# One PSUM tile with named banks, k projected by 64-row tiles, and a fixed instruction order computed anew

## Chip, cores, metric

One core of one Trainium2 chip. The metric is device time in microseconds (us) of one execution. A kernel is run several times; the median is quoted. Ratios and their 95% intervals compare the fast runs alone: the mean time of one kernel's fast runs over that of the other's of the same rounds, so not quite the ratio of the medians. The profile names the engines PE (TensorE matmul), PEld (its weight loads), DVE (VectorE), ACT (ScalarE), POOL (GpSimd) and SP (SyncE, which only issues transfers here).

## The reference

Two parts, joined. First an attention without softmax over 64 (batch, head) pairs of 576 rows by 64, then a two-layer net on the 4608 rows:

```python
def phi(x):                                   # x: [8, 8, 576, 64], w_phi: [64, 128]
    proj = np.einsum('bhsd,df->bhsf', x, w_phi)
    proj = proj - np.max(np.abs(proj), axis=-1, keepdims=True)
    return np.concatenate([np.exp(proj), np.exp(-proj)], axis=-1)
q_p, k_p = phi(q), phi(k)
kv  = einsum('bhsf,bhsd->bhfd', k_p, v);  z = sum(k_p, axis=2)
attn = einsum('bhsf,bhfd->bhsd', q_p, kv) / (einsum('bhsf,bhf->bhs', q_p, z)[..., None] + 1e-06)
x = attn as [4608, 512]
h = x @ w_in                                  # [4608, 2048]
out = where(h > 0, h, exp(min(h, 0)) - 1) @ w_out
```

## The kernel before

It is a list of small steps, each a Python function with a one-letter name. A string of 1709 letters fixes in which order the steps are recorded, and with it the order on each engine. In the profile of before these steps start in that order: the 272 of C, N, s and V on VectorE, the 251 of E, r, e, f and g on GpSimd, the 420 of B, D, T, q and u on ScalarE, and A, M, U, W, p and t on TensorE. There a waiting step held up those behind it: GpSimd stood still for 4.1 us ahead of the q load issued at 21.06 us, and the scalings of v behind that load began only at 22 us. The pairs of heads are taken in 16 groups n of four heads; two groups make a batch. The 4608 rows of the second part are taken in 9 chunks.

The steps that load constants, those that copy the transposes of the first groups, and their transposes of m and x on TensorE (a to d, k, m, P, Q, Y, Z) are left out of this table.

| letter | step | engine |
|---|---|---|
| e, f, g, h, i | load k, q, v, w_in, w_out (casting, issued by GpSimd) | POOL |
| j, l / n, o | transpose k, q on TensorE (groups 0 to 3) / by a transposing transfer | PE / SP |
| A, B, C | pk = k times w_phi; its two exps; its maximum mk | PE, ACT, DVE |
| D, E, F | em = exp of mk; vs = v times em; its column of ones | ACT, POOL |
| M, N, O, R | pm = q times w_phi; its maximum mq; split in two bf16 (mhl; on POOL in the first groups); transpose it to mT by a transfer | PE, DVE, POOL, SP |
| S, T | pq = q times w_phi less the maximum (by way of mT); its two exps | PE, ACT |
| U, V, W, X, z | kv; its copy; pn; division; transpose to xT by a transfer | PE, DVE, SP |
| p, q, r, s | ph = x @ w_in; exp; min; the sum of both into gT | PE, ACT, POOL, DVE |
| t, u, v | po = gT @ w_out; copy; store | PE, ACT, SP |

PSUM is given out by two pools: two places of two banks and four places of one bank.

```python
pjp = ctx.enter_context(tc.tile_pool(name="pjp", bufs=2, space=bass.MemoryType.PSUM))   # pk, pm, pq, kv, pn
mpp = ctx.enter_context(tc.tile_pool(name="mpp", bufs=4, space=bass.MemoryType.PSUM))   # ph, po, transposes
...
w_bd = consts.tile([P, 2, F], BF16)           # block-diagonal: w_phi for rows 0-63 | for rows 64-127
...
def k_mm(n, c):
    pj = two_banks([P, 8, F], FP32, "pk")
    for i3 in range(3):
        nc.tensor.matmul(                     # 128 rows, 256 columns; half of the weight is zero
            pj[:, 2 * i3:2 * i3 + 2, :].rearrange("p r f -> p (r f)"),
            st["kT", n][:, 3 * c + i3, :], w_bd.rearrange("p r f -> p (r f)"), start=True, stop=True)
    st["pk", n, c] = pj[:, 0:6, :]

def m_mm(n, c):                               # q already goes by two 64-row tiles, side by side
    ...
    for j in range(p1 - p0):
        for par in range(2):
            rows = slice(par * D, (par + 1) * D)
            nc.tensor.matmul(pj[:, par, j, :], st["qT", n][rows, ..., :], w_bd[rows, par, :], ...)
...
for letter in "".join(ORDER.split()):
    fn, args = queues[letter]
    fn(*next(args))
```

Of the kernel before, what the change touches and what calls it, by code (L numbers as in the profile page):

```python
# [8 lines left out]
FP32 = mybir.dt.float32  # L10
# [6 lines left out]
ORDER = """  # L17
eabecedjfkfAjgBhkBAhCeBjfABkjiBCliBlkAmDgmlCBFlemBAmDfCBFBMNECEMNDAOEPBQMENBFCSEDUETTFEMVOENPWQM
XOgPQNYMZSNOUTTjVjSkWkTPjXjTlAQkYkBSZlemlTpCTpqWmqrBrspspXqMqrprqNMrNSTsMsTpsYNqprAZqOSBsrtmTsCP
lTpWmqQBfpXpDrqFMqrNrABsMstsBNEYpCMqEpNDAqrBZSrsFpBsOpEnqpCTtrqEsqSTprTrSssTpopTUTqVAqrqrCWrsDsB  # L20
tEsXBpFPpEuQWzqqprXrpqvSqrsTrAszpsTtsCqzSrsDpTEzppBtEnTtBFgMqtqNrqrrUsussvMVppNqWqrpsrXMqprpqszS
sqrpNeTtzrqsTsrAOtsBoWBRtXtCzAutCzAtDCBEvtBFtEnDBMFupNEBvpqESqMrpTNfTpsrqMsqSrpTNrTpsqOSsRqUrTrs
oTtVsAWBpXBpqCzArqpCrzWqsBXrpDBEsAzqsSEBtzTCprTnFspDqEMBpNrqSqFsMrTNrpTEsMqSspeToNTgpOqrRtqrsUrs
sAVtBWBtXutvCWztXAztBtzBtuCzftDvEtMEuMNpvFNpqrSqAsTprnCTpqsDSrBpFsETpBEpTMqUNqrqrsSqroVTprsTWOsq
RWXrppXzqArqsAzBrspBszpsBCpzqBrpqsAqrCpnBrsDSBEspTCFtETDSqEMtNTETtqMFSqgNtoTrTUrsuesMvtVrNWtsOWX
RtXzAtBzABtBCztuCtzADtBECntuFEvDMBtNFvBEtAESBtfTCtTtBuSAvTtCTtDBEMpNuFBvpEqMqSrNpTorsTpOsqRUqrrs
ApVBnspBpqCqrWqrsSDrpXTFETpszqsMESqNpzTrTprsqMgsMqpNrpeqsrNSqproTsrWTOpsqRsrpqXrUqszrAstBsztVBWC
tXWtXfzMutNzMtNzSSTztTtvTATtCuMtDvNBEpBFAEqAnpBrpBOsRBtCqtCqrDArsupBFCvEpqsBArpCnqEBtsrBUsDBEtVD
qFFSEWTotXTrtEszWuESXzpTgTpvqMMqzrNprNpqzsrMqSspTrNTpsqSOqsrURTrsTpsoVpqWrqsSrpTXTpszqSqrWTzrtsT
XtsMzMtNtzNMutNvtORAABpBpBCpqCtqrqrAsDtBnrCpFuEsBAvspEqCBprBpsDBEAtCqFqArtqCnrBtrsDDEstBstBFFEuU  # L30
BvEtVEAWBpEXBpqCzprqsArzqUCrsDpBEspVqFBEpqSrqSoTrtsTrspsTWTpXqprqzsrSqMstTrzNTtusSvMTtNTotMWNtXW
utOzXAtBzABtzBCtBztDCuEARtBFMvEBpNvpCqrMqpNDrSsqFUETsTpEVMqrpNrSsqSTstrTOspRTWTtXqWrupzXSqztsTrT
SsztTzTSpTvpTqpqrAqtrsBrspBspqCprqsDtrqFspEupvqrEpsqtrqrtsrsUstVtWuWXvtXtztztztutztvttupvpqprqst
rqsprspqprqstrqsprspqprqstrqspruspvqprqsprqsprqsprqsprqsprqsprqsprqsprqsprqsprqstrqsprspqprqstrq
sprspqprqstrqsprspqprqstrqsprustvqtrstttutvtttutvtttutvtttutvtttutvtttutvttuv
"""
# [3 lines left out]
def kernel(  # L40
# [43 lines left out]
    opool = ctx.enter_context(tc.tile_pool(name="opool", bufs=3))  # L84
    pjp = ctx.enter_context(tc.tile_pool(name="pjp", bufs=2, space=bass.MemoryType.PSUM))
    mpp = ctx.enter_context(tc.tile_pool(name="mpp", bufs=4, space=bass.MemoryType.PSUM))

    ctx.enter_context(tc.manual_schedule(engines=None))

    def two_banks(shape, dtype, name):  # L90
        return pjp.tile(shape, dtype, name=name, tag="pj")

    def one_bank(shape, dtype, name):
        return mpp.tile(shape, dtype, name=name, tag="mp")

    ident = consts.tile([P, P], BF16)
    w_bd = consts.tile([P, 2, F], BF16)
    sel_small = consts.tile([P, NI], BF16)
# [61 lines left out]
    def weights():  # L160

        nc.vector.memset(w_bd, 0.0)
        nc.vector.memset(sel_small, 0.0)
        for j in range(2):
            nc.vector.memset(mhl[j], 0.0)
        for par in range(2):
            r = slice(par * D, (par + 1) * D)
            nc.vector.tensor_copy(w_bd[r, par, :], st["w_f32"][r, :])

# [56 lines left out]

    def k_mm(n, c):
        pj = two_banks([P, 8, F], FP32, "pk")
        for i3 in range(3):
            nc.tensor.matmul(  # L230
                pj[:, 2 * i3:2 * i3 + 2, :].rearrange("p r f -> p (r f)"),
                st["kT", n][:, 3 * c + i3, :],
                w_bd.rearrange("p r f -> p (r f)"),
                start=True,
                stop=True,
            )
        st["pk", n, c] = pj[:, 0:6, :]

    def k_exp(n, c, sg):
        EK = get(("EK", n), lambda: work.tile([P, 2, 2 * NS, F], BF16, name="EK"))  # L240
        nc.scalar.activation(  # L241
            EK[:, sg, 6 * c:6 * c + 6, :], st["pk", n, c], ACT.Exp,
            scale=1.0 - 2.0 * sg,
        )

    def k_max(n, c):
        mk = get(("mk", n), lambda: small.tile([P, 2 * NS], FP32, name="mk"))
        nc.vector.tensor_reduce(  # L248
            mk[:, 6 * c:6 * c + 6], st["pk", n, c], axis=AX.X, op=ALU.max,
            apply_absolute_value=True,  # L250
        )
# [25 lines left out]

    def m_mm(n, c):
        own = min(n // FIRST, 1)
        p0, p1 = PIECES[own][c]  # L280
        pj = two_banks([P, 2, 4, P], FP32, "pm")
        for j in range(p1 - p0):
            for par in range(2):
                rows = slice(par * D, (par + 1) * D)
                nc.tensor.matmul(  # L285
                    pj[:, par, j, :],
                    st["qT", n][rows, PLACE_OF[own][par][p0 + j], :],
                    w_bd[rows, par, :],
                    start=True,
                    stop=True,  # L290
                )
        st["pm", n, c] = pj
# [231 lines left out]

    def o_mm(ch, tt, part):
        po = get(("po", ch, tt), lambda: one_bank([P, DM], FP32, "po"))
        for jt in range(4 * part, 4 * part + 4):
            nc.tensor.matmul(  # L528
                po,
                st["gT", ch][:, jt, tt * P:(tt + 1) * P],  # L530
                w_out_sb[:, jt, :],
                start=(jt == 0),
                stop=(jt == N_JT - 1),
            )
# [107 lines left out]
```

## Time and profile before

The first measurement of before was 397.58 us (median of 3; 395.66 to 401.7). The profile comes from a run of 400.01 us.

| what | profile before |
|---|---|
| span | 398.2 us |
| TensorE busy | 364.5 us, 92% |
| first ph | 42.4 us (in three variants with the same head: 41.2 to 41.6) |
| TensorE at 160 to 200 us | busy without a gap (40.00 of 40 us) |
| pk against pm | see the two rows below |

Two rows of the groups of TensorE's instructions, kept apart by shape. The columns are line, engine, operation, names, rows used and shape, count, then busy time in us and mean ns of one, then idle time before it with its releasers.

```profile
L230 PE MATMUL pk<-w_bd,kT 128*128 128x256 bf16 x144 | 24.7, 285 | 5.2 <-DVE kT L214 2.0 <-DVE mk L248 1.4 <-DVE xp L446 1.4
L285 PE MATMUL pm<-w_bd,qT 64*128 64x128 bf16 x288 | 16.2, 224 | 3.5 <-DVE mq L297 2.0 <-DVE mk L248 1.1 <-DVE xp L446 0.3
```

Both do the same arithmetic on arrays of the same size, k and q. The 64-row form has twice the instructions and two thirds of the busy time.

### The profile page before, as it was taken

What the parts mean: (1) busy time and instruction counts of PE and PEld (TensorE: products, weight loads), DVE (VectorE), ACT (ScalarE), POOL (GpSimd) and SP (SyncE); (2) the same over time, 40 slices, a digit from 0 to 9 for tenths busy, and PEclk for the clock granted to TensorE, in tenths of its full rate; (3) what the DMA queues carried; (4) which work ended last, traced back from release to release, by engine and by line L of the source; (5) the groups of instructions that cost most, each with busy time, mean ns of one, the idle gap of its engine ahead of it and who ended that gap; (6) DMA issues with size and microseconds to landing.
All of it is one profiled execution on the core that took longest, in us unless ns stands there. A gap on an engine that the chain in (4) does not pass through costs nothing.

```text
span 398.2 us, 9735 instructions
## 1 busy us (share of the span) xinstructions
PE 364.5 (92%) x3928; PEld 199.4 (50%) x3928; DVE 244.0 (61%) x427; ACT 248.7 (62%) x453; POOL 194.1 (49%) x309
## 2 busy tenths in 40 slices
PE   3548889989999699999999999999999999999995
PEld 2336666654646254545564555555555454444442
DVE  4825996665886259654995767766767551585100
ACT  3722778757894288579856977597767932565211
POOL 8383366636492355654733763297235350575100
PEclk9955999999999789999999999999999999999999
DMA  7999992699739923798398674241531215000233
GB/s 100 204 207 208 208 174 49 81 151 153 104 59 158 152 49 60 114 179 163 50 167 142 91 124 72 47 93 38 96 64 35 56 29 111 10 16 2 56 77 79
DMA packets 69565, 40.09 MB, mean 101 GB/s; under 512 B 49936, under 2 KB 64400, under 8 KB 69520
## 3 DMA queue, kind: packets, MB, share of 16 engines
q1 hardware_dynamic: 54176, 21.12, 31.2%
q0 software_dynamic: 15344, 18.35, 29.6%
q8 instruction: 31, 0.51, 0.5%
q14 instruction: 14, 0.11, 0.1%
HBM read 36.77 MB, written 9.44 MB: 116 GB/s over the span
## 4 chain that ended last, share of the span: by engine, by line
PE 74%; DMA 10%; POOL 6%; DVE 5%; issue 2%; ACT 2%; SPq 0%; POOLq 0%; ACTq 0%
PE po L528 28%; PE ph L500 28%; PE pn L429 4%; PE kv L398 4%; DMA w_in_sb<-in_moe_w_in_dram 3%; DMA xT_sb<-xp 3%; PE pk L230 3%; POOL vs L266 3%; PE pq L359 2%; DMA kT<-kn 2%; PE pm L285 2%; PE pq L369 2%; DVE xp L446 1%; DVE gT L520 1%; DVE mq L297 1%
## 5 line engine op out<-in xcount | busy, mean ns | idle before, releaser
L500 PE MATMUL ph<-xT_sb,w_in_sb 128*128 128x512 bf16 (+1 forms) x640 | 140.2, 362 | 4.9 <-DMA xT_sb<-xp 4.3
L516 POOL TENSOR_SCALAR e_sb<-e_sb 128x512 f32<-128x512 f32 (+1 forms) x160 | 90.4, 573 | 106.7 <-ACT e_sb L511 105.9
L528 PE MATMUL po<-w_out_sb,gT 128*128 128x512 bf16 x576 | 137.3, 379 | 0.5 <-DVE gT L520 0.5
L520 DVE SCALAR_TENSOR_TENSOR gT<-e_sb,ph 128x512 bf16<-128x512 f32 (+1 forms) x160 | 97.2, 629 | 47.2 <-POOL e_sb L516 46.4
L511 ACT ACTIVATE e_sb<-ph 128x512 f32<-128x512 f32 (+1 forms) x160 | 86.5, 567 | 39.7 <-PE ph L500 36.6
L241 ACT ACTIVATE EK<-pk 128x768 bf16<-128x768 f32 x96 | 74.1, 814 | 27.8 <-PE pk L230 27.7
L266 POOL TENSOR_TENSOR vs<-vn,em 128x576 bf16<-128x576 bf16 x64 | 73.0, 1154 | 36.4 <-ACT em L257 32.0
L500 PEld LDWEIGHTS <-w_in_sb 128*128 128x128 bf16 x640 | 59.3, 98 | 62.1 <-issue 6.5
L528 PEld LDWEIGHTS <-gT 128*128 128x128 bf16 x576 | 53.4, 98 | 57.8 <-DVE gT L520 1.6
L381 ACT ACTIVATE Eq<-pq 128x768 bf16<-128x768 f32 (+2 forms) x96 | 72.4, 819 | 15.2 <-PE pq L369 14.8
L297 DVE TENSOR_REDUCE mq<-pm 128x6 f32<-128x768 f32 (+2 forms) x48 | 45.4, 953 | 24.5 <-PE pm L285 24.4
L248 DVE TENSOR_REDUCE mk<-pk 128x6 f32<-128x768 f32 x48 | 45.3, 953 | 19.7 <-ACT EK L241 11.2
L538 ACT COPY o_sb<-po 128x512 f32<-128x512 f32 x36 | 21.2, 590 | 47.6 <-PE po L528 46.4
L230 PE MATMUL pk<-w_bd,kT 128*128 128x256 bf16 x144 | 24.7, 285 | 5.2 <-DVE kT L214 2.0
L446 DVE TENSOR_TENSOR xp<-pn,rec 128x640 bf16<-128x640 f32 (+2 forms) x32 | 26.4, 824 | 1.1
L429 PEld LDWEIGHTS <-Eq 128*128 128x128 bf16 x640 | 24.0, 98 | 5.7 <-issue 1.1
L429 PE MATMUL pn<-kv_sb,Eq 128*128 128x65 bf16 x640 | 25.4, 195 | 0.4 <-DVE kv_sb L409 0.4
L398 PEld LDWEIGHTS <-EK 64*128 64x128 bf16 x1152 | 21.3, 99 | 3.9 <-issue 1.3
L398 PE MATMUL kv<-vs,EK 64*128 64x65 bf16 x1152 | 22.8, 197 | 0.0
L230 PEld LDWEIGHTS <-kT 128*128 128x128 bf16 x144 | 13.1, 100 | 15.5 <-DVE xp L446 3.2
L285 PE MATMUL pm<-w_bd,qT 64*128 64x128 bf16 x288 | 16.2, 224 | 3.5 <-DVE mq L297 2.0
L257 ACT ACTIVATE em<-mk 128x9 f32<-128x9 f32 x64 | 10.1, 219 | 14.5 <-DVE mk L248 14.4
(44 smaller groups left out, 159.5 us busy)
## 6 DMA issues: line engine op xcount, KB each, us to landing
out_dram<-o_sb SPq DMA_DIRECT2D x72, 128.0 KB, 2.4
vn<-in_v_dram POOLq DMA_DIRECT2D x8, 576.0 KB, 9.3
kn<-in_k_dram POOLq DMA_DIRECT2D x7, 576.0 KB, 11.1
qn<-in_q_dram POOLq DMA_DIRECT2D x7, 576.0 KB, 8.1
w_in_sb<-in_moe_w_in_dram POOLq DMA_DIRECT2D x2, 1024.0 KB, 15.5
w_out_sb<-in_moe_w_out_dram POOLq DMA_DIRECT2D x2, 1024.0 KB, 28.9
xT_sb<-xp SPq DMA_TRANSPOSE x56, 2.7
qn<-in_q_dram POOLq DMA_DIRECT2D x2, 288.0 KB, 6.2
```

Source lines behind the costliest of these rows:

```text
L230: nc.tensor.matmul(pj[:, 2 * i3:2 * i3 + 2, :].rearrange("p r f -> p (r f)"), st["kT", n][:, 3 * c + i3, :], w_bd.rearrange("p r f -> p (r ...
L241: nc.scalar.activation(EK[:, sg, 6 * c:6 * c + 6, :], st["pk", n, c], ACT.Exp, scale=1.0 - 2.0 * sg,)
L266: nc.gpsimd.tensor_tensor(get(("vs", n), new_vs)[:, sg, r, 0:D], st["v", n // 2][:, 2 * (n % 2) + pr], st["em", n][:, sg, r].unsqueeze(2). ...
L297: nc.vector.tensor_reduce(mq[:, :, p0:p1], st["pm", n, c][:, :, 0:p1 - p0, :], axis=AX.X, op=ALU.max, apply_absolute_value=True,)
L381: nc.scalar.activation(Eq[:, sg, :, :, p0 * D:p1 * D].rearrange("p h r x -> p r h x"), st["pq", n, c][:, :, 0:(p1 - p0) * P].rearrange("p ...
L398: nc.tensor.matmul(kv[:, hi, pr, sg, :], EK[rows, sg, pr * NS + s, :], vs[rows, sg, pr * NS + s, :], start=(s == 0), stop=(s == NS - 1),)
L429: nc.tensor.matmul(pn[:, hi, x, :], Eq[:, sg, hi, par, i0 * D:(i0 + 2) * D], kv_sb[:, hi, pr, sg, :], start=(sg == 0), stop=(sg == 1),)
L500: nc.tensor.matmul(ph, w_in_sb[:, ct, jt * P:(jt + 1) * P], xT_sb[:, ct, ch * CHUNK + h0:ch * CHUNK + h1], start=(ct == 0), stop=(ct == N_ ...
L511: nc.scalar.activation(e_sb, st["ph", ch, jt, h0], ACT.Exp)
L516: nc.gpsimd.tensor_scalar(e_sb, e_sb, 1.0, 0.0, op0=ALU.min, op1=ALU.max)
L520: nc.vector.scalar_tensor_tensor(gT[:, jt, h0:h1], st["e", ch, jt, h0], -1.0, st["ph", ch, jt, h0], op0=ALU.add, op1=ALU.max,)
L528: nc.tensor.matmul(po, st["gT", ch][:, jt, tt * P:(tt + 1) * P], w_out_sb[:, jt, :], start=(jt == 0), stop=(jt == N_JT - 1),)
```

## The change

Its intent is threefold. PSUM becomes one tile of 8 banks, and each TensorE step in the order carries a digit that names its bank (the first of two for pairs). k is projected as q was, in pairs of 64-row tiles that write to two banks. The order is computed anew, with TensorE work placed between the issue of a transfer and its first use.

```diff
-    pjp = ctx.enter_context(tc.tile_pool(name="pjp", bufs=2, space=bass.MemoryType.PSUM))
-    mpp = ctx.enter_context(tc.tile_pool(name="mpp", bufs=4, space=bass.MemoryType.PSUM))
+    psum = ctx.enter_context(
+        tc.tile_pool(name="psum", bufs=1, space=bass.MemoryType.PSUM)
+    ).tile([P, 8, 512], FP32, name="banks")
 ...
-    w_bd = consts.tile([P, 2, F], BF16)
+    w_sb = consts.tile([P, F], BF16)
 ...
-    def k_mm(n, c):
-        pj = two_banks([P, 8, F], FP32, "pk")
+    def k_mm(n, c, bank=None):
+        pj = two_banks(bank).rearrange("p r (i f) -> p r i f", f=F)
         for i3 in range(3):
-            nc.tensor.matmul(pj[:, 2 * i3:2 * i3 + 2, :]..., st["kT", n][:, 3 * c + i3, :], w_bd..., ...)
+            for par in range(2):
+                rows = slice(par * D, (par + 1) * D)
+                nc.tensor.matmul(pj[:, par, i3, :], st["kT", n][rows, 3 * c + i3, :], w_sb[rows, :], ...)
 ...
-    for letter in "".join(ORDER.split()):
+    for letter, bank in re.findall(r"([A-Za-z])(\d?)", "".join(ORDER.split())):
         fn, args = queues[letter]
-        fn(*next(args))
+        fn(*next(args), **({"bank": int(bank)} if bank else {}))
```

The first line of the order, before and after (26 more lines of it are left out):

```diff
-eabecedjfkfAjgBhkBAhCeBjfABkjiBCliBlkAmDgmlCBFlemBAmDfCBFBMNECEMNDAOEPBQMENBFCSEDUETTFEMVOENPWQM
+eabeecj7fdfkA0gj7BhkBhj6CA2eA4Bkj7fA0kBil6Bl7CiBmgl3mBl6CDBmFM4mA2DCA6FBENM0BEBNM4BECM0ECDM2NDM6
```

More of the change, by code (lines that the diff above doesn't have):

```diff
@@ L2 @@
+import re
 from contextlib import ExitStack
@@ L17 @@
 ORDER = """
-eabecedjfkfAjgBhkBAhCeBjfABkjiBCliBlkAmDgmlCBFlemBAmDfCBFBMNECEMNDAOEPBQMENBFCSEDUETTFEMVOENPWQM
-XOgPQNYMZSNOUTTjVjSkWkTPjXjTlAQkYkBSZlemlTpCTpqWmqrBrspspXqMqrprqNMrNSTsMsTpsYNqprAZqOSBsrtmTsCP
-lTpWmqQBfpXpDrqFMqrNrABsMstsBNEYpCMqEpNDAqrBZSrsFpBsOpEnqpCTtrqEsqSTprTrSssTpopTUTqVAqrqrCWrsDsB
-tEsXBpFPpEuQWzqqprXrpqvSqrsTrAszpsTtsCqzSrsDpTEzppBtEnTtBFgMqtqNrqrrUsussvMVppNqWqrpsrXMqprpqszS
-sqrpNeTtzrqsTsrAOtsBoWBRtXtCzAutCzAtDCBEvtBFtEnDBMFupNEBvpqESqMrpTNfTpsrqMsqSrpTNrTpsqOSsRqUrTrs
@@ L23 @@
-oTtVsAWBpXBpqCzArqpCrzWqsBXrpDBEsAzqsSEBtzTCprTnFspDqEMBpNrqSqFsMrTNrpTEsMqSspeToNTgpOqrRtqrsUrs
-sAVtBWBtXutvCWztXAztBtzBtuCzftDvEtMEuMNpvFNpqrSqAsTprnCTpqsDSrBpFsETpBEpTMqUNqrqrsSqroVTprsTWOsq
-RWXrppXzqArqsAzBrspBszpsBCpzqBrpqsAqrCpnBrsDSBEspTCFtETDSqEMtNTETtqMFSqgNtoTrTUrsuesMvtVrNWtsOWX
-RtXzAtBzABtBCztuCtzADtBECntuFEvDMBtNFvBEtAESBtfTCtTtBuSAvTtCTtDBEMpNuFBvpEqMqSrNpTorsTpOsqRUqrrs
-ApVBnspBpqCqrWqrsSDrpXTFETpszqsMESqNpzTrTprsqMgsMqpNrpeqsrNSqproTsrWTOpsqRsrpqXrUqszrAstBsztVBWC
-tXWtXfzMutNzMtNzSSTztTtvTATtCuMtDvNBEpBFAEqAnpBrpBOsRBtCqtCqrDArsupBFCvEpqsBArpCnqEBtsrBUsDBEtVD
@@ L29 @@
-qFFSEWTotXTrtEszWuESXzpTgTpvqMMqzrNprNpqzsrMqSspTrNTpsqSOqsrURTrsTpsoVpqWrqsSrpTXTpszqSqrWTzrtsT
-XtsMzMtNtzNMutNvtORAABpBpBCpqCtqrqrAsDtBnrCpFuEsBAvspEqCBprBpsDBEAtCqFqArtqCnrBtrsDDEstBstBFFEuU
-BvEtVEAWBpEXBpqCzprqsArzqUCrsDpBEspVqFBEpqSrqSoTrtsTrspsTWTpXqprqzsrSqMstTrzNTtusSvMTtNTotMWNtXW
-utOzXAtBzABtzBCtBztDCuEARtBFMvEBpNvpCqrMqpNDrSsqFUETsTpEVMqrpNrSsqSTstrTOspRTWTtXqWrupzXSqztsTrT
-SsztTzTSpTvpTqpqrAqtrsBrspBspqCprqsDtrqFspEupvqrEpsqtrqrtsrsUstVtWuWXvtXtztztztutztvttupvpqprqst
-rqsprspqprqstrqsprspqprqstrqspruspvqprqsprqsprqsprqsprqsprqsprqsprqsprqsprqsprqstrqsprspqprqstrq
@@ L35 @@
-sprspqprqstrqsprspqprqstrqsprustvqtrstttutvtttutvtttutvtttutvtttutvtttutvttuv
+eabeecj7fdfkA0gj7BhkBhj6CA2eA4Bkj7fA0kBil6Bl7CiBmgl3mBl6CDBmFM4mA2DCA6FBENM0BEBNM4BECM0ECDM2NDM6
+OFENU4NENEP7VEQS0FOU2TOeTfgW0VP7P6XOP5QQY4j7Zj6kS0kS2QTj7A4kj6TCTkW0l7BXl6TY1Bl0ZeS2p1mTmA4Tp7Cq
+M2qrp6NrDBFsM2qsBp1Nrl7qM4srW2Np6XOA4qBrsBP3Y2sp1QZp6qCS2qrTrsS4sp1DmTp6Fmp0TM2Tp7NqW4qrqrsqS2rX
+p1rTETsY5sEqp4sM2ZqS6ENp0Tp5TnEM2NqS6qrTU2rsOsTrrsP4p1fVp7qsp6oqrQp5sqrA2sqrA0Cp4rp7qsBrsp6Cqp5B
+rsqsW2Brp7sqXp4Brp6qp1qsrzqW2rsqrDsp5rXp7zEqp4qp0sEzA2sqp6Cqt1FzrDrstBEsnqtBEtFS2rurst7TrsvsTM0S
@@ new lines @@
+4NgtTTM0M2NtNS4U0ToeOTA2VtRBt6uCW0vBtXtzA0A2BW4ztXBt7BnCutBztDCEzM0S4NDM2tTEvNTM0ENuS2S4TvA6EA0T
+oFTFp3fOCTRp2CqBp5rqsp4qrBp3rsqsU6qrBrsp5DVBEp4sqW0Eqp7Xrp6qrszW0rqsp5Frszp4Xqp7rqszrA0sqM2p6Czr
+p5sqnBsrp4Nqt7BrsqS2sM0Drp6TNFETtsqM0ES2NS4TtorTOU0sTReTA2VtgBt6uCW0vBtXM2S4NztTTW0fzA2XA4BtnBt7
+BzCM0tuCDzS2ENtDTvEtBM0TES4Nt6ToETtuFtFOvU0A2RA4VBtBW0p7uXBvp6qCp1Bzrqp3sqzrCp7qrsDp5rqsEp6sqW0r
+qrA2sp4BnrXp7EBszqp1FCqrp5qzrsDM2rsqp0ENp6qsrp4sqEsS2qp7FTrt5TrsrsqM0S2gstTNrTp6esM0qS2NtTorOTU0
+sRA2A6VBtBW0t4BXutBCvW0CtzXA2DA5BEtzBA0Ft7zEBCtuzCDM2EtCBvtENDnBS4FuM2Et6NTvtETBS2FM4fTtNTS0OU4R
@@ new lines @@
+TTA2VtoBW0uCnp7XDp6vBEW4qzEqp3Xp2rzqrsp5qzrsp7qrszFsM0qrS3Np6TgTsp2reqsp5qrM0qS3rsp7TrNTp6sqsM0S
+2qrNp4oTrsTp5sqU0OqrRrA2sA6BVp4Bsp1qCBp5rqsW2qrCt4rXDtBEtszFsEM2A0NW6zBftXBnt5uCS2zS6TM0tNDzTEtT
+vtFETS0uM2A6oTNt4TCtvOU0BRBA2Vp5BW0qCA6rtnXDBEtBszt3EuCtzFDtBEvW0Ep7XtFqzrM0uS4Np6TzgsTS0M2vTp7N
+TM4S2Nqp1oTrp5TOsRqp4qrp6qrsqp3rsqrsp7qrsp5rqsp4rsqsp6rqsrA0qA2Cp7rsp5Bsqp4Cqrt6BrsBtsqU0BrDsA2E
+tBnVS4BFS0ETtCTt7TW2TW4XDtuEXtvES0zM2M4TFNtTzNt6utzM0A2zA4NBtOBvU0BCRtBVA2uoCt7BW0DvCW4Ep6XnDBEt
+qXzEp3zS0FqEM4tTNzTFtrrszM0uS4Np2TvsTS0M6Tp3oNTA4OU6CqRqrp1VBrsp0Bsqp7qrp6qrsp5rsqsW1rqp4srXW6qp
@@ new lines @@
+3rszM0sqp2Nrzp5qXp4rqszp7rqsrS0qszM2p6TNrTt5sqsS0rS2TtsTtTM0TA6NtBA2Out4CRtCDvBEtBFtEDBt7uEtvEA0
+A2A4Bp6FBtBCtqCU0ruCDvBEt7VBtsEDBW0EW2XS4EtTXzTtFFzS0uS2TU4zTp7VTzp6Tvqp5qrp4qrsW0rsqW2srp7Xp6qX
+zp5rqsp1rzqsp4rqszt7rsqsztrsp6p5qp4rqsp3rqsp6rqsp5rqstrqsp4rsp6qtrqst5rustvttt7utvttp6up5vqp7rqs
+p4rqsp6rqsp5rqsp7rqst4rqstrsttt7utvp6p5qp4rqsp3rqsp6rqsp5rqstrqsp4rsp6qp5rqsp3rqstrqst6rustvttt7
+utvttp6up5vqp7rqst4rqstrsttp7up6vqp5rqsp4rqsp7rqsp6rqsp5rqsp4rqsp7rqsp6rqst5rqstrsttt7utvttt6utv
+ttt7utvttuv
@@ L84, with two_banks, transposes @@
     opool = ctx.enter_context(tc.tile_pool(name="opool", bufs=3))
-    pjp = ctx.enter_context(tc.tile_pool(name="pjp", bufs=2, space=bass.MemoryType.PSUM))
-    mpp = ctx.enter_context(tc.tile_pool(name="mpp", bufs=4, space=bass.MemoryType.PSUM))
+    psum = ctx.enter_context(
+        tc.tile_pool(name="psum", bufs=1, space=bass.MemoryType.PSUM)
+    ).tile([P, 8, 512], FP32, name="banks")
     ctx.enter_context(tc.manual_schedule(engines=None))
-    def two_banks(shape, dtype, name):
-        return pjp.tile(shape, dtype, name=name, tag="pj")
-    def one_bank(shape, dtype, name):
-        return mpp.tile(shape, dtype, name=name, tag="mp")
+    def two_banks(bank):
+        return psum[:, bank:bank + 2, :]
+    def transposes(bank):
+        return psum[:, bank, :].bitcast(BF16).rearrange("p (j c) -> p j c", c=P)
     ident = consts.tile([P, P], BF16)
-    w_bd = consts.tile([P, 2, F], BF16)
+    w_sb = consts.tile([P, F], BF16)
     sel_small = consts.tile([P, NI], BF16)
@@ L160, in weights @@
     def weights():
-        nc.vector.memset(w_bd, 0.0)
         nc.vector.memset(sel_small, 0.0)
@@ L165, in weights @@
             nc.vector.memset(mhl[j], 0.0)
-        for par in range(2):
-            r = slice(par * D, (par + 1) * D)
-            nc.vector.tensor_copy(w_bd[r, par, :], st["w_f32"][r, :])
+        nc.vector.tensor_copy(w_sb, st["w_f32"])
     def selectors():
@@ L198, in load_w_out, with t_pe @@
         nc.gpsimd.dma_start(out=w_out_sb[:, c, :], in_=w_out_r[:, c, :])
-    def t_pe(name, n, j0, j1):
+    def t_pe(name, n, j0, j1, bank=None):
         nat = st[name, n // 2][:, 2 * (n % 2):2 * (n % 2) + 2].rearrange(
@@ L204, in t_pe @@
         )
-        tr = one_bank([P, 8, P], BF16, "tr")
+        tr = transposes(bank)
         for j in range(j0, j1):
@@ L224, in t_dma @@
         )
-    def k_mm(n, c):
-        pj = two_banks([P, 8, F], FP32, "pk")
+    def k_mm(n, c, bank=None):
+        pj = two_banks(bank).rearrange("p r (i f) -> p r i f", f=F)
         for i3 in range(3):
-            nc.tensor.matmul(
-                pj[:, 2 * i3:2 * i3 + 2, :].rearrange("p r f -> p (r f)"),
-                st["kT", n][:, 3 * c + i3, :],
-                w_bd.rearrange("p r f -> p (r f)"),
-                start=True,
-                stop=True,
-            )
-        st["pk", n, c] = pj[:, 0:6, :]
+            for par in range(2):
+                rows = slice(par * D, (par + 1) * D)
+                nc.tensor.matmul(
+                    pj[:, par, i3, :],
+                    st["kT", n][rows, 3 * c + i3, :],
+                    w_sb[rows, :],
+                    start=True,
+                    stop=True,
+                )
+        st["pk", n, c] = pj[:, :, 0:3, :]
     def k_exp(n, c, sg):
@@ L241, in k_exp @@
         nc.scalar.activation(
-            EK[:, sg, 6 * c:6 * c + 6, :], st["pk", n, c], ACT.Exp,
-            scale=1.0 - 2.0 * sg,
+            EK[:, sg, 6 * c:6 * c + 6, :].rearrange("p (i r) f -> p r i f", r=2),
+            st["pk", n, c], ACT.Exp, scale=1.0 - 2.0 * sg,
         )
@@ L248, in k_max @@
         nc.vector.tensor_reduce(
-            mk[:, 6 * c:6 * c + 6], st["pk", n, c], axis=AX.X, op=ALU.max,
+            mk[:, 6 * c:6 * c + 6].rearrange("p (i r) -> p r i", r=2),
+            st["pk", n, c], axis=AX.X, op=ALU.max,
             apply_absolute_value=True,
@@ L275, in v_ones, with m_mm @@
         nc.gpsimd.tensor_copy(get(("vs", n), new_vs)[:, :, r, D], st["em", n][:, :, r])
-    def m_mm(n, c):
+    def m_mm(n, c, bank=None):
         own = min(n // FIRST, 1)
         p0, p1 = PIECES[own][c]
-        pj = two_banks([P, 2, 4, P], FP32, "pm")
+        pj = two_banks(bank).rearrange("p r (i f) -> p r i f", f=F)
         for j in range(p1 - p0):
@@ L287, in m_mm @@
                     st["qT", n][rows, PLACE_OF[own][par][p0 + j], :],
-                    w_bd[rows, par, :],
+                    w_sb[rows, :],
                     start=True,
@@ L313, in m_split, with m_pe @@
         )
-    def m_pe(n, part):
-        tr = one_bank([P, 8, P], BF16, "tr")
+    def m_pe(n, part, bank=None):
+        tr = transposes(bank)
         nc.tensor.transpose(tr[:, 0, :], mhl[n % 2].rearrange("p r x -> p (r x)"), ident)
@@ L328, in m_dma, with q_mm @@
         )
-    def q_mm(n, c):
+    def q_mm(n, c, bank=None):
         own = min(n // FIRST, 1)
@@ L335, in q_mm @@
         qT, mT = st["qT", n], st["mT", n]
-        pj = two_banks([P, 2, 4 * P], FP32, "pq")
+        pj = two_banks(bank)
         runs = []
@@ L360, in q_mm @@
                     places(par, j, m),
-                    w_bd[rows, par, :],
+                    w_sb[rows, :],
                     qT[rows, i:i + m, :].rearrange("p i (h t) -> p h i t", h=2),
@@ L386, in q_exp, with kv_mm @@
         )
-    def kv_mm(n):
+    def kv_mm(n, bank=None):
         EK, vs = st["EK", n], st["vs", n]
-        pj = two_banks([P, 2, 512], FP32, "kv")
+        pj = two_banks(bank)
         kv = pj[:, :, 0:4 * (D + 1)].rearrange("p h (r g d) -> p h r g d", r=2, g=2)
@@ L418, in x_parts, with x_mm @@
         return [(part, t) for t in range(5)]
-    def x_mm(n, part):
+    def x_mm(n, part, bank=None):
         Eq, kv_sb = st["Eq", n], st["kv", n]
         parts = x_parts(n, part)
-        pj = two_banks([P, 2, 512], FP32, "pn")
+        pj = two_banks(bank)
         pn = pj[:, :, 0:len(parts) * (D + 1)].rearrange("p h (x d) -> p h x d", d=D + 1)
@@ L452, in x_div, with x_pe @@
         st["xp", n, part] = xp
-    def x_pe(n, part):
+    def x_pe(n, part, bank=None):
         xp = st["xp", n, part]
-        tr = one_bank([P, 8, P], BF16, "trx")
+        tr = transposes(bank)
         for x in range(len(x_parts(n, part))):
@@ L494, in x_dma, with h_mm @@
             )
-    def h_mm(ch, jt, h0, h1):
-        ph = one_bank([P, CHUNK], FP32, "ph")[:, h0:h1]
+    def h_mm(ch, jt, h0, h1, bank=None):
+        ph = psum[:, bank, h0:h1]
         for ct in range(N_CT):
@@ L523, in h_elu, with o_mm @@
         )
-    def o_mm(ch, tt, part):
-        po = get(("po", ch, tt), lambda: one_bank([P, DM], FP32, "po"))
+    def o_mm(ch, tt, part, bank=None):
+        po = get(("po", ch, tt), lambda: psum[:, bank, :])
         for jt in range(4 * part, 4 * part + 4):
```

## The prediction

> **What bounds the kernel now.** I read the page first (shares, slices), then the busy time by stretches of 20 us, then the chain of waits, then TensorE's order of time.
>
> ```profile
> PE 364.5 (92%) x3928; PEld 199.4 (50%) x3928; DVE 244.0 (61%) x427; ACT 248.7 (62%) x453; POOL 194.1 (49%) x309
> ...
> PE   3548889989999699999999999999999999999995
> PEclk9955999999999789999999999999999999999999
> ```
>
> TensorE is busy 92% of the span. The slices show where it is not: slices 1 to 4 (0 to 40 us) and slice 14 (130 to 140 us), each with a halved clock in or after it. By stretches:
>
> ```profile
> 20.00:40.00 20.00, 12.57 (x251) 10.16 (x252) 8.17 (x17) 5.21 (x9) 12.33 (x21) 0.52 1.19 208
> 120.00:140.00 20.00, 16.54 (x188) 8.63 (x187) 9.05 (x16) 6.91 (x14) 5.39 (x8) 0.87 1.13 152
> 160.00:180.00 20.00, 20.00 (x235) 10.70 (x229) 12.46 (x20) 12.77 (x24) 11.36 (x15) 1.00 0.91 141
> ```
>
> From 160 us on TensorE has no idle (20.00 of 20) at full clock, and no other engine comes near: there only less TensorE work helps. In the head all is waiting. The chain of waits says for what:
>
> ```profile
> 7.12 13.41 DMA w_in_sb<-in_moe_w_in_dram
> 21.06 0.74 POOL qn L185
> 22.07 2.15 POOL vs L266 x2
> 24.64 2.21 POOL vs L266 x2
> 27.06 2.15 POOL vs L266 x2
> 29.42 1.05 POOL vs L266
> ...
> 35.37 2.05 PE kv L398 x72
> ...
> 127.90 8.19 DMA xT_sb<-xp
> 136.13 2.29 PE ph L500 x5
> ```
>
> GpSimd sits in front of a q load of the third batch (its issue at 21.06 waited 4.1 us for the first half of w_in to land), and only behind it scales v (vs), which the kv matmuls need. So the head's bound is the order of GpSimd's queue, not arithmetic. At 127.90 a transposing transfer of xT takes 8.19 us while the ph that needs it is next in TensorE's queue. The prices of small steps come from TensorE's order of time, start to start:
>
> ```profile
> 213.27 1.90 PE L528 MATMUL po<-w_out_sb,gT 128*128 128x512 bf16 x8
> 215.01 0.49 PE L230 MATMUL pk<-w_bd,kT 128*128 128x256 bf16 x3
> 215.33 1.03 PE L528 MATMUL po<-w_out_sb,gT 128*128 128x512 bf16 x4
> 216.29 0.34 PE L285 MATMUL pm<-w_bd,qT 64*128 64x128 bf16 x6
> 216.57 1.04 PE L528 MATMUL po<-w_out_sb,gT 128*128 128x512 bf16 x4
> 217.44 1.03 PE L500 MATMUL ph<-xT_sb,w_in_sb 128*128 128x512 bf16 x4
> ```
>
> A pk step takes 0.32 to 0.33 us. Four po take 0.87 (216.57 to 217.44) where a 128-row step follows, but 0.96 (215.33 to 216.29) where the 64-row pm follows. The pm step takes 0.28, although two pq steps in a row elsewhere show 0.16 to 0.17 for six such matmuls. So each change between 128-row and 64-row tiles costs about 0.105 us.
>
> [...]
>
> **The change part by part.**
> (1) k by 64-row tiles. The old step streams 3 x 256 columns against a half-empty block-diagonal weight. The new one streams three pairs of 128 columns, two at a time: as a pm step, 0.165 us without changes of mode. 48 steps save 48 x (0.33 - 0.165) = 7.9 us. Alone between 128-row steps it would cost 0.165 + 0.21 = 0.375, more than before, so the order decides. I counted the changes of mode in both order strings: 158 before; 164 after; 216 if only k were changed and the old order kept; 130 for the new order with the old k. So the whole costs 6 x 0.105 = 0.6 us in changes and saves 7.3 us; k alone in the old order would save just 7.9 - 6.1 = 1.8 us. ScalarE and VectorE read as many elements as before (814 against 819 ns, 953 against 953 for the like-shaped steps of q): nothing there.
> (2) All TensorE work, from such durations: before, ph 110.5 + 14.0 (the halves of chunk 0), po 124.3, pn 20.1, kv 18.4, pk 15.8, pm 7.9, pq 15.8, transposes 98 x 0.056 = 5.5, changes of mode 16.6: 348.9 us. After: 341.6 us.
> (3) The head. The first ph starts at 42.4 us before, with 13.8 us of this work done ahead of it. In the new order GpSimd's queue has the third batch's loads behind all eight scalings of v, so the first scaling waits only for em and v. Em of the first group is ready about 14 us; the v load, issued at 6.4, at a median of 9.3 us lands about 15.7. Eight scalings of 1.15 us from 15.7 on, with the small steps between them, end at about 26; the second kv before started at 35.1 with the last scaling ending at 32.0 and some queueing. From second kv to first ph was 7.3 us before. So the first ph comes at about 26 + 7.5 = 33.5; I take 34, since the q load of the second batch lands at about 30[...].
> (4) Room behind transfers, counted as TensorE work in the order between issue and first use. xT to the first ph of chunk 2 had 3.1 us and now 10.0; chunks 4 to 7 had 2.6 to 5.0, now 5.9 to 13.6; mT to its first use was as low as 2.6, now 3.8 at least. Chunk 1 stays at 3.1. The wait at chunk 2 was 1.05 + 2.40 = 3.5 us idle, and 2.6 us more went in the 5.2 us of half clock after it: 6 us come back. Chunk 1's wait (1.4 us) stays.
> (5) Named banks. Pairs may now stand on four places instead of two and single banks on all eight. Before, TensorE waited for a bank's reader 8.3 us in the whole run (the waits of pm, pk and pq for mq, mk, xp and Eq), 4.9 of it in the first 43 us, so by itself this is worth 1 to 3 us, already inside the head's figure.
>
> **The sum.** Before: 42.4 + (348.9 - 13.8) = 377.5; the last matmul ends at 393.6, so 16.1 us went after the head; tail to the span's end 4.6, span to reported time 1.8: 400.0, the profiled run. After: 13.1 us of work lie ahead of the first ph, so 34 + (341.6 - 13.1) = 362.5; plus 16.1 - 6 = 10.1; plus 4.6 + 1.8: 379. The profiled run of before was 2.4 us above the median of 397.58; half of that off gives **378 us**.
>
> **Rivals.**
> A: The head does not move, since the loads bind it: 204 to 208 GB/s stand in every slice from 10 to 50 us, and w_in, the second batch's k and q must land anyway. For: the DMA queues are full then. Against: w_in landed by 25 us (longest 17.6 us after 7.8), long before its first use at 42.4. Then only (1) and (4) stay: 13 us, 385 to 387.
> B: A wait moves. The new order was computed, and GpSimd and VectorE are strict queues: with the head 8 us earlier, the second batch's v (issued behind w_out, landing at about 42) may now be late for its scaling, and h_min steps stand behind it in the queue; VectorE was at 19.15 of 20 us between 40 and 60. For: this stretch has the least slack. Against: the order has some 11 us of TensorE work between the first ph and that scaling, so it falls at 45. It would cost 2 to 5 us: 380 to 383.
> C: [...] each pair does not overlap: then (1) saves nothing, 385. Against: pm has the very same form and does overlap.
> D: All waits of the middle vanish, also those of banks: 16 us become 5, 372.
>
> **Range and chances.** The least sure term is the head (4 to 11 us), then the middle (2 to 10), then k (5 to 8). The smallest of all gives 387, the largest 369. I take 371 to 387. A gain under 2% would be over 389.6: for that head and middle must both fail. Faster 0.93, same 0.06, slower 0.01.
>
> **What would show it.** Right: pk becomes 288 matmuls of 64x128 at about 216 ns, busy time near pm's 16.2 against 24.7 us; changes of mode still 0.105; the first ph at about 34 us; no 4 us wait of GpSimd for w_in; no half clock near 138 us; TensorE full from about 60 us. Wrong: first ph at 40 or later, TensorE idle for over 10 us after it, or GpSimd waiting for v of the second batch with ph waiting for banks.

## The result, and the profile after

The changed kernel took 381.46 us (median of 4 runs, 379.34 to 382.61). Its ratio to before is 0.9614, 95% interval 0.9548 to 0.968. Two further measurements, on two different chips, gave 0.9679 (0.9643 to 0.9714) and 0.9588 (0.9536 to 0.9639). So about 15 us were gained. The profile is of a run of 380.56 us, span 378.7 us.

From the page: TensorE's share and slices, and its granted clock.

```profile
PE 352.2 (93%) x4072; PEld 192.0 (51%) x4072; DVE 244.5 (65%) x425; ACT 251.8 (66%) x453; POOL 193.8 (51%) x309
...
PE   2767889998997999999999999999999999999995
PEclk9999999999999999999999999999999999999999
```

TensorE is busy for 12.3 us less, and slices 2 and 3 have filled in part (from 5 and 4 tenths to 7 and 6). No slice shows a halved clock. The record of the clock begins at 24.0 us in this run, though; durations before that are those of a halved clock: nine transposes took 1.14 us at 11.10 us and 0.68 at 29.13 us. In before nine took 1.14 us at 37.35 us under a recorded 0.5, and 0.67 at 39.74 us under 1.0. Another profile of the same kernel, after_third, shows 0.89 and 0.85 in its first two stretches of 20 us, and a halved clock from 118.1 to 121.5 us.

By stretches of 20 us (busy time of PE, PEld, DVE, ACT, POOL with counts, then clock, DMA share, GB/s):

```profile
20.00:40.00 20.00, 14.73 (x321) 11.53 (x321) 14.47 (x32) 10.68 (x18) 10.91 (x23) 1.00 1.19 207
100.00:120.00 20.00, 17.55 (x245) 9.46 (x244) 14.07 (x24) 13.49 (x23) 8.88 (x13) 1.00 0.74 112
120.00:140.00 20.00, 20.00 (x229) 10.29 (x228) 13.04 (x22) 15.95 (x31) 10.79 (x15) 1.00 0.72 128
```

From 120 us to the last matmul TensorE is idle for 0.1 us in all (before it was full from 160 us on, but for 0.3 us). The hole at 130 to 140 us is gone, but a smaller one stands at 100 to 120 us. The chain of waits names both the new head and the new hole:

```profile
6.33 9.04 DMA vn<-in_v_dram
...
15.45 4.48 POOL vs L272 x4
...
20.55 4.37 POOL vs L272 x4
...
110.05 7.31 DMA mT<-mhl
```

The scalings of v begin when v has landed, at 15.45 us, not when w_in has (22.0 us before). The hole at 115 us is a transfer of mT that took 7.31 us. TensorE's order of time, start to start, shows the first ph and the price of k steps:

```profile
35.28 0.61 PE L506 MATMUL banks<-xT_sb,w_in_sb 128*128 128x256 bf16 x4
35.83 0.34 PE L235 MATMUL banks<-w_sb,kT 64*128 64x128 bf16 x6
36.10 0.61 PE L506 MATMUL banks<-xT_sb,w_in_sb 128*128 128x256 bf16 x4
...
199.27 0.33 PE L291 MATMUL banks<-w_sb,qT 64*128 64x128 bf16 x6
199.44 0.33 PE L235 MATMUL banks<-w_sb,kT 64*128 64x128 bf16 x6
199.70 1.90 PE L534 MATMUL banks<-w_out_sb,gT 128*128 128x512 bf16 x8
```

Alone between ph steps, a k step takes 0.27 us and lengthens the ph before it from 0.44 to 0.55: 0.38 in all for itself, no gain over 0.33. Behind a pm step (199.27) the pm takes 0.17 and the k step 0.26, of which 0.1 is the way back to 128 rows. Their line by shape:

```profile
L291 PE MATMUL banks<-w_sb,qT 64*128 64x128 bf16 x288 | 16.9, 228 | 3.3 <-DVE mq L303 1.8 <-DVE mk L253 1.5
...
L235 PE MATMUL banks<-w_sb,kT 64*128 64x128 bf16 x288 | 14.9, 228 | 1.2 <-DVE kT L217 1.2
```

k's busy time fell from 24.7 to 14.9 us, at the same 228 ns as pm.

### The profile page after: what moved, and what is told of

The parts are those of the page before. It is cut to its first block, busy times and chain, and to the rows that moved or that the text cites. A ratio compares the mean times of both kernels' runs of the same rounds, so it can differ in the third digit from the quotient of the medians.

```text
span 378.7 us, 10054 instructions
## 1 busy us (share of the span) xinstructions
PE 352.2 (93%) x4072; PEld 192.0 (51%) x4072; DVE 244.5 (65%) x425; ACT 251.8 (66%) x453; POOL 193.8 (51%) x309
## 4 chain that ended last, share of the span: by engine, by line
PE 79%; POOL 7%; DMA 4%; DVE 3%; ACT 3%; issue 2%; POOLq 0%; ACTq 0%; DVEq 0%
PE banks L534 33%; PE banks L506 30%; PE banks L435 5%; PE banks L404 4%; POOL vs L272 4%; DMA vn<-in_v_dram 2%; PE banks L365 2%; DMA mT<-mhl 2%; PE banks L291 2%; PE banks L235 2%; PE banks L375 2%; DVE mq L303 1%; ACT Eq L387 1%; POOL e_sb L522 1%; ACT e_sb L517 1%
## 5 line engine op out<-in xcount | busy, mean ns | idle before, releaser
L506 PE MATMUL banks<-xT_sb,w_in_sb 128*128 128x512 bf16 (+1 forms) x640 | 134.6, 358 | 1.2 <-ACT Eq L387 0.9
L534 PE MATMUL banks<-w_out_sb,gT 128*128 128x512 bf16 x576 | 134.8, 380 | 0.0
L526 DVE SCALAR_TENSOR_TENSOR gT<-e_sb,banks 128x512 bf16<-128x512 f32 (+1 forms) x160 | 97.0, 630 | 50.2 <-POOL e_sb L522 49.4
L517 ACT ACTIVATE e_sb<-banks 128x512 f32<-128x512 f32 (+1 forms) x160 | 87.2, 565 | 40.1 <-PE banks L506 34.4
L246 ACT ACTIVATE EK<-banks 128x768 bf16<-128x768 f32 x96 | 74.8, 818 | 20.5 <-PE banks L235 16.3
L387 ACT ACTIVATE Eq<-banks 128x768 bf16<-128x768 f32 (+2 forms) x96 | 72.0, 812 | 21.1 <-PE banks L375 20.2
L303 DVE TENSOR_REDUCE mq<-banks 128x6 f32<-128x768 f32 (+2 forms) x48 | 45.1, 954 | 16.7 <-PE banks L291 14.2
L253 DVE TENSOR_REDUCE mk<-banks 128x6 f32<-128x768 f32 x48 | 45.0, 953 | 11.4 <-ACT EK L246 11.2
L452 DVE TENSOR_TENSOR xp<-banks,rec 128x640 bf16<-128x640 f32 (+2 forms) x32 | 26.4, 824 | 1.1
L435 PE MATMUL banks<-kv_sb,Eq 128*128 128x65 bf16 x640 | 24.6, 193 | 1.5 <-ACT Eq L387 1.0
L415 DVE CAST kv_sb<-banks 128x520 bf16<-128x520 f32 x16 | 11.2, 697 | 11.6 <-PE banks L404 11.5
L375 PE MATMUL banks<-mT,sel 64*128 64x128 bf16 x288 | 16.1, 218 | 2.6 <-DMA mT<-mhl 2.5
L291 PEld LDWEIGHTS <-qT 64*128 64x128 bf16 x288 | 9.7, 98 | 14.9 <-issue 14.4
```

The source lines that it names most:

```text
L246: nc.scalar.activation(EK[:, sg, 6 * c:6 * c + 6, :].rearrange("p (i r) f -> p r i f", r=2), st["pk", n, c], ACT.Exp, scale=1.0 - 2.0 * sg,)
L253: nc.vector.tensor_reduce(mk[:, 6 * c:6 * c + 6].rearrange("p (i r) -> p r i", r=2), st["pk", n, c], axis=AX.X, op=ALU.max, apply_absolute ...
L303: nc.vector.tensor_reduce(mq[:, :, p0:p1], st["pm", n, c][:, :, 0:p1 - p0, :], axis=AX.X, op=ALU.max, apply_absolute_value=True,)
L387: nc.scalar.activation(Eq[:, sg, :, :, p0 * D:p1 * D].rearrange("p h r x -> p r h x"), st["pq", n, c][:, :, 0:(p1 - p0) * P].rearrange("p ...
L435: nc.tensor.matmul(pn[:, hi, x, :], Eq[:, sg, hi, par, i0 * D:(i0 + 2) * D], kv_sb[:, hi, pr, sg, :], start=(sg == 0), stop=(sg == 1),)
L506: nc.tensor.matmul(ph, w_in_sb[:, ct, jt * P:(jt + 1) * P], xT_sb[:, ct, ch * CHUNK + h0:ch * CHUNK + h1], start=(ct == 0), stop=(ct == N_ ...
```

## The experiments

Kernels are compared only within the same rounds. The rows of letters in the diffs below are order strings cut to the place that was edited. All outputs are right.

### The yardstick

> The changed kernel once more, as the yardstick for the runs beside it. Every theory: 380 to 383 us, about 0.96 of the kernel before; first ph at 35.3 us, last matmul at about 374 us.

> The changed kernel again as the yardstick on this chip: 380 to 383 us, ratio to before 0.961 to 0.968.

Measured: 382.47 us (ratio 0.9679) and 381.62 us (0.9588). Mean times of fast runs are 382.04 and 381.57 us. First ph at 35.5 and 34.9 us. The two ratios differ by 0.9%, more than each interval's half width. Before, on these two chips, had means of 394.9 and 397.8 us.

### k back to 128 rows in the new order

```diff
-    for par in range(2): matmul(pj[:, par, i3, :], kT[rows, ...], w_sb[rows, :])
+    matmul(pj[:, 2 * i3:2 * i3 + 2, :], kT[:, ...], w_bd)      # same order, same banks
```

> The changed kernel with k projected as before (three matmuls of 128 rows by 256 columns against the block-diagonal weight), same order, same banks. My theory: streams cost 48 x 0.165 = 7.9 us more, and changes of mode fall from 164 to 130, 34 x 0.105 = 3.6 us less, so 4.3 us longer than the changed kernel (385 to 387 us). Rival 1, [...]: 7.9 us longer. Rival 2, the pairs don't overlap or TensorE is not the bound: no difference (within 1 us).

Measured: 385.15 us, ratio 0.9758 (0.9727 to 0.9788). That is 3.1 us over the changed kernel by means (385.16 against 382.04). My 4.3 is within the intervals; 7.9 and 0 are not. So the 64-row tiles do save, and less than their streams alone. Where the rest goes can be read in a stretch without waits. From the twentieth k step to the last matmul both kernels ran at full clock and TensorE was idle for at most 0.1 us: 257.6 us here, 254.8 in the changed kernel. The 29 k steps of this stretch stream 29 x 0.165 = 4.8 us more, but only 2.8 us more passed. This run has 18 changes of mode fewer there, so each is worth 2.0 / 18 = 0.11 us: the price that the prediction had read from single steps.

### k by 64 rows in the old order

```diff
-            matmul(pj[:, 2 * i3:2 * i3 + 2, :], kT[:, ...], w_bd)
+            for par in range(2): matmul(pj[:, par, i3, :], kT[rows, ...], w_bd[rows, par, :])   # in the old pools
```

> The kernel before with k projected by 64-row tiles, nothing else: old order, old pools. My theory: the streams save 7.9 us, changes of mode rise from 158 to 216 (58 x 0.105 = 6.1 us), so 1.8 us faster than before (ratio about 0.995). Rival 1, the 64-row tiles carry the gain whatever the order: 7 to 8 us faster. Rival 2, changes of mode cost more where k stands among wide matmuls: slower.

Measured: 395.62 us, ratio 0.9998 (0.9944 to 1.0053), no gain. The interval holds my 1.8 us and excludes the 7 to 8 us of the rival. So the same edit that is worth 3 us in the new order is worth nothing that could be measured in the old one. There 27 of the 48 k steps stand alone among 128-row steps, in the new order 11. The profiles agree: from the 27th k step to the last matmul, idle time taken off, the 128-row form took 220.2 to 220.4 us in the old order (before, old_queue, old_xT) and the 64-row form 219.8, though its streams are shorter by 22 x 0.165 = 3.6 us.

### The head: GpSimd's queue put back in the new order

```diff
-...CDBmFM4mA2DC...OU2TOeTfgW0...
+...CDBmFefM4mA2DC...OU2TOTgW0...
```

> The changed kernel with the third batch's k and q loads put back ahead of the eight first scalings of v in GpSimd's queue (where they were before). My theory of the head: GpSimd waits for w_in again until about 21 us, the scalings come some 6 us later, the first ph moves from 35.3 to about 41 us and the whole takes 5 to 7 us more (387 us). Rival, the head was made faster by TensorE's order and the named banks, or the loads bind it: within 1 us of the changed kernel.

Measured: 389.08 us, ratio 0.9853 (0.9821 to 0.9885): 6.9 us over the changed kernel by means (388.91 against 382.04), at the upper end of what was expected. The order of time of GpSimd shows the cause (the bracket is idle time and its releaser):

```profile
21.69 0.74 POOL L188 DMA_DIRECT2D qn<-in_q_dram  x1 [5.33 <-DMA w_in_sb<-in_moe_w_in_dram]
22.43 0.27 POOL L281 CAST vs<-em 128x18 bf16<-128x18 f32 x1
22.59 4.48 POOL L272 TENSOR_TENSOR vs<-vn,em 128x576 bf16<-128x576 bf16 x4
```

Two letters bring back the old wait for w_in; the scalings start at 22.6 and the first ph at 43.4 us, 7.9 us later than in the changed kernel on this chip (I had expected about 41). This part of the head's theory is shown.

### The head: the same two letters in the old order

```diff
-...DgmlCBFlemBAmDfCBFBMNE...TTFEMVOENPWQM...
+...DgmlCBFlmBAmDCBFBMNE...TTFEMVOEefNPWQM...
```

> The kernel before with the third batch's k and q loads moved behind the eight first scalings of v in GpSimd's queue, nothing else. My theory: the wait for w_in at 16.9 to 21 us goes, the scalings start at about 15.5 instead of 22 us, the first ph at about 36 instead of 42.4 us, and the whole is 5 to 7 us faster (ratio 0.982 to 0.987). Rival, the loads bind the head, or old pools hold TensorE back there: under 2 us.

Measured: 392.92 us, ratio 0.9934 (0.9877 to 0.9991): between 0.4 and 4.9 us faster, short of my 5 to 7. The first ph came at 36.9 us, against 41.2 to 41.6 in the three fast profiles with the old head. So the first ph came some 4.5 us earlier, a gain which the interval includes; I had counted from the slow profile's 42.4 and hoped for 36.

### Room for xT in the old order

```diff
-...MEuMNpvFNpqrSq...       (the tile's t t t t u v stand about 110 letters later)
+...MEuMNttttuvpvFNpqrSq...
```

> The kernel before with the last output tile of chunk 1 (four po steps, copy and store) moved ahead of the first ph of chunk 2, so that the xT transfer before it has 6.6 instead of 3.1 us of TensorE work to hide behind; 4 changes of mode fewer. My theory: of the 3.5 us idle at 132 to 136 us about 1 stays, the half clock after it goes (2.6 us), 0.4 us for the modes: 4 to 5.5 us faster (ratio 0.986 to 0.990). Rival, TensorE is filled there but the po steps are missed later, where they filled a wait: under 2 us.

Measured: 395.79 us, ratio 0.9998 (0.9949 to 1.0047): nothing, where I had expected 4 to 5.5 us. By stretches:

```profile
120.00:140.00 20.00, 20.00 (x153) 10.01 (x152) 9.54 (x15) 10.55 (x20) 6.41 (x10) 1.00 1.07 168
140.00:160.00 20.00, 17.25 (x292) 10.24 (x289) 15.18 (x26) 17.99 (x33) 13.82 (x20) 1.00 0.39 59
```

The profile of before was of a slow run, so I compare with that of old_k64, a fast run with the same order in this part:

```profile
120.00:140.00 20.00, 17.86 (x140) 8.24 (x139) 9.63 (x16) 9.95 (x19) 6.36 (x10) 0.91 0.92 153
140.00:160.00 20.00, 19.49 (x282) 10.43 (x282) 15.15 (x26) 18.20 (x34) 13.81 (x20) 1.00 0.35 49
```

The hole at 120 to 140 us is closed (20.00 busy, full clock; 17.86 at 0.91 in old_k64). A new one stands at 140 to 160 us: 17.25 busy, against 19.49. There the po steps that I had taken away used to fill the time in which pm and pq wait for VectorE and ScalarE. The rival was right: moving filler work from one hole to another gained nothing here.

### Room for mT in the new order, twice

```diff
 new_mT    -...M2S4NztTTW0fzA2XA4BtnBt7BzCM0t...
           +...M2NztW0fzA2XA4BtnBt7BzCS0TTM0t...
 new_mT2:  letter o (qT of group 7) from ahead of R (mT of group 6) to behind it;
           M2 N of group 7 from ahead of S4 to ahead of M0
```

> The changed kernel with the first pq step of group 6 (and its two exps) moved behind one pn, two pk and three po steps, so that its mT transfer, which took 7.3 us and left TensorE idle for 2.45 us, has room. If room behind transfers is what keeps TensorE full: the idle time goes and the whole is 2 to 3 us shorter (378.5 to 379.5 us). Rival, the wait moves to another place since VectorE or ScalarE have no slack, or the transfer comes later too: within 1 us of the changed kernel.

> The changed kernel with the mT transfer of group 6 issued ahead of group 7's qT transfer on the same queue (not behind it), and group 7's first pm step moved to just ahead of its second so that qT has room in turn. In the first try the wait moved to a bank that pq had just taken; here no bank is taken at short notice. If transfers are the wait: no idle for mT or qT near 115 us, 2 to 3 us shorter than the changed kernel. If the place only hides another wait: as the first try, 1.7 us or less.

Measured, first try: 380.69 us, 1.7 us under the changed kernel by means (380.38 against 382.04; ratios 0.9636 and 0.9679, whose intervals overlap). The wait for mT went, and most of it came back at another place. One row of the order of time of each kernel, the changed one first:

```profile
117.40 0.34 PE L375 MATMUL banks<-mT,sel 64*128 64x128 bf16 x6 [2.45 <-DMA mT<-mhl]
```

```profile
121.31 0.34 PE L291 MATMUL banks<-w_sb,qT 64*128 64x128 bf16 x6 [1.65 <-ACT Eq L387]
```

In the second row TensorE waits for the exps to leave bank 0, the bank I had given to the moved step: the very next pm step wanted it. Second try: 380.55 us, ratio 0.9573 against the changed kernel's 0.9588, or 0.6 us by means: the two are not told apart. Its mT was issued first on the queue at 111.4 us and was still awaited until 117.9 us, with TensorE idle for 1.49 us. So qT ahead of it on the queue was not what made mT slow. In the changed kernel the input loads of k, v and q were issued at 109.4, 110.3 and 112.4 us, just beside it, and DMA moved 128 and then 232 GB/s in the two stretches of 4 us from 112 us on. That these loads slow it down fits, but no run removed them; it stays open.

### Banks alone, in the old order

```diff
-  PSUM: two pools (2 places of two banks, 4 of one)
+  PSUM: one tile of 8 banks, each step on the place that was freed longest ago; order and 128-row k kept
```

> The kernel before, its order letter for letter and k in 128-row form, but PSUM as one tile of 8 banks, each step on the place that was freed longest ago. If the old order had no use for more banks (too-early reuses counted after the first ph: 9.6 us with pools, 10.1 so): no change, within 1 us of before. If banks alone are worth something, as my prediction had it: 1 to 3 us faster.

Measured: 399.28 us, ratio 1.0023 (0.9967 to 1.0079): no gain. The interval excludes all but the lowest end of 1 to 3 us. The old order was made for pools and shows no use for more.

### The new order on the old places

```diff
-  digits 0 to 7 as in the changed kernel
+  pairs only on 0-1 and 2-3, single banks only on 4 to 7; TensorE's sequence kept, four swaps of neighbours on VectorE
```

> The changed kernel with every engine's sequence kept (TensorE's wholly, VectorE's but for four swaps of neighbours), but with PSUM used as before: pairs only in two places, single banks only in the four others. In the new order four pairs or six single banks hold data at once at times, so steps must wait for readers. Counted in the order, bank reuses that come sooner than the readers need add up to 61 us after the first ph, against 16 us in the changed kernel (which really lost 10 us there to all waits). If the named banks are what the new order stands on: 15 to 40 us longer than the changed kernel, at or over the time of before. If banks are worth 1 to 3 us, as my prediction put it: 382 to 386 us.

Measured: 446.66 us, ratio 1.1295 (1.1233 to 1.1357): some 66 us over the changed kernel (0.1295 + 0.0373, the mean shortfall of its three ratios from 1, is 0.167 of 396.3 us). The expected 15 to 40 was too little. The longest waits of TensorE are for readers of banks:

```profile
PE banks L506 <- DVE gT L526: 7.2, 14, 1.4
PE banks L235 <- DVE mk L253: 6.2, 4, 2.5
PE banks L291 <- DMA qT<-qn: 5.6, 1, 5.6
...
PE banks L235 <- ACT Eq L387: 4.1, 6, 1.3
PE banks L291 <- ACT Eq L387: 3.9, 5, 1.7
```

(Columns: who waited for whom, us in total, times, longest.) They are spread over ph, pk and pm. A single long wait, such as that for qT, may be a consequence: what comes late delays its transfer as well. Nor is all of the loss idle time: the first ph came at 43.8 us (35.3 in the changed kernel's profile), TensorE was idle for 51 us after it (7.4), and its clock was halved for 25 us of that part (never). This run does not say that banks are worth 66 us. An order computed for six places would do better, as the old one shows. It says that this order cannot be had on the old places.

### All parts but the new order

```diff
+  64-row k, one tile of 8 banks (freed longest ago), the two letters behind the scalings, the room for xT
   in the old order otherwise
```

> Everything but the new order: 64-row k, named banks (freed longest ago), the old order with the two loads behind the scalings and with room for xT at chunk 2; 212 changes of mode. If the parts add up as they did singly (0, -2.6, 0, and 0 to -2 for banks): 2 to 5 us faster than before (ratio about 0.99). If they unlock one another: 8 us or more (ratio 0.98 or less). The rest up to the changed kernel's 0.965 is what the order computed anew adds.

Measured: 393.12 us, ratio 0.9876 (0.9831 to 0.9921): 4.9 us faster than before (3.1 to 6.7). The single parts as measured sum to about 2 us (0.1, 2.6, 0.1 and -0.9), each uncertain by about 2. So the 8 us of parts that unlock one another are excluded; whether they help each other a little, these runs can't tell. The changed kernel in the same call had 0.9588. So 11.5 us (393.04 less 381.57, means) of the 16.4 come only with the order computed anew. Of these, 48 fewer changes of mode (212 against 164) are 48 x 0.105 = 5.0 us by my price. The first ph is at 36.4 against 34.9 us. The rest, some 5 us, can be found after the first ph. There TensorE was idle for 15.0 us in the profile of this kernel and 11.9 in the changed one's, and its clock was halved for 6.8 against 3.4 us, which I estimate at 1.7 us more, half of the difference: a pk step of before took 0.62 us under the halved clock (139.11 us) and 0.32 at full clock (126.52 us). That makes about 5 us in all. (Both profiles lack some 50 matmul records, which makes the idle time look a little longer.) The largest differences stand at two places: TensorE was busy 18.16 and 16.66 of 20 us at 60 to 80 and 140 to 160 us, against 19.63 and 19.47 in the changed kernel's.

## Why the prediction was right, point by point

**The time.** 378 us were predicted, 371 to 387 as range; 381.5 was measured. The gain was foreseen at about 20 us and came out at about 15. The sum started from a slow run of before (400.0 us, against means of 394.9 to 397.8), of which only 1.2 us was taken off.

**Sum and term.** The sum held in the profile. The last matmul ended at 374.05 us, and the first ph came at 35.28 (said: 34). Without the 328.5 us of computed work, 10.3 us are left (said: 10.1 of waits). TensorE was idle for 7.4 of them; the others are work that took longer than its price. The prices can be checked where TensorE hardly waits: from the k step at 119.27 us in the changed kernel to the end the order counts 254.0 us; the profile took 254.8.

**(1) k and the changes of mode.** Right in mechanism and sign. Putting the old form back costs 3.1 us where 4.3 was computed, and the new form alone in the old order gives 0 where 1.8 was computed, both within their intervals. This pair of runs says that the order decides, though by time alone the two gains are only just told apart; the stretches without waits say it more clearly (2.8 us for 29 k steps in the new order, about 0.5 us for 22 in the old one). There the price of 0.105 us, read from single steps, is confirmed at 0.11.

**(3) The head.** Right: the first ph at 35.3 us, no wait of GpSimd for w_in, and putting back two letters costs 6.9 us. Rival A (the loads bind the head) is refuted by that run. The reckoning of the first ph was in part lucky, though. I had the second kv at 26 us and the first ph 7.5 us later. In the profile the second kv began at 24.0 us and the first ph followed 11.3 us later: on the chain of waits, GpSimd issues three loads (25.9 to 28.1 us) ahead of the split of mq that TensorE waits for.

**(4) Room behind transfers.** The step "6 us come back" held as a sum (16.1 to 10.3 us) and failed in its place. The wait at chunk 2 did go, and the 6.8 us of halved clock at that place with it. But a wait for mT of group 6 came, with 2.0 to 2.5 us of idle time in the three profiles, and in one of them (after_third) the clock was halved for 3.4 us right behind it. So TensorE was not full from about 60 us, as said: it was idle for 3.5 us between 80 and 120 us. I had counted this very room (3.8 us) and passed over it because it was larger than the smallest of before (2.6 us). What counts is the transfer at that place, 7.3 us against a median of 4.2. And old_xT shows that room given at one place alone is worth nothing if the work that makes it is missed elsewhere. That the total still came to 10.3 us is luck in how the terms fell: 3.8 us of them were idle time between 36 and 60 us, where VectorE was the busiest engine (17.67 of 20 us). That is the half of rival B that came true.

**The clock.** The record of before has the clock halved from 18.6 to 39.1 and from 134.7 to 141.5 us. In the 4 us ahead of the two, TensorE was busy for 1.1 and 2.0 us, and until the halving it was idle for at most 1.3 us at a time. So at both places several short waits close together came first. What halves the clock is not shown.

**(5) Named banks.** This is the term that was worst mis-sized, in a way that the sum could not show. I wrote that banks are "worth 1 to 3 us" by themselves. By themselves they gained nothing that could be measured (old_banks: between 1.3 us faster and 3.1 us slower). As a condition of the new order they are needed: on the old places it is 66 us slower. I treated the parts as terms that add. They are not: banks give little or nothing by themselves, they allow an order which groups the 64-row steps and keeps up to four pairs of banks full at once.

**What stays open.** Some 5 us of the 11.5 us that only the order gives are located as idle time and halved clock, not traced to single waits. The slow mT is not explained beyond its neighbours.

## What to carry to other kernels

When several edits come together with a new order, first ask which of them are gains and which only make the order possible: test each both by adding it alone to the old kernel and by taking it alone from the new one, and expect the two to differ. Count the changes between 128-row and 64-row tiles in the order before splitting a matmul into row tiles; here each costs about 0.105 us, so a lone 64-row step of six matmuls (0.38 us) lost against the full-row one (0.33), and a step beside others of its kind won (0.26 behind a pm step, the way back included). Where an engine takes its steps in the order of the program, as here, look for what stands ahead of critical work and waits for something unrelated: two letters in GpSimd's queue were worth 7 us in the new order, and 0.4 to 4.9 in the old one.
